# Attention ahead of two mixture-of-experts layers: the maxima are turned behind the next pair's scores, and the transfers and pieces around them move

## The chip, the cores and the metric

The kernel runs on one core of one Trainium2 chip. A core has five engines that run their own instruction lists: PE (TensorE, matrix products), DVE (VectorE), ACT (ScalarE), POOL (GpSimd) and SP (SyncE, which here issues nearly all DMA transfers, one behind the other). The metric is device time in microseconds (us) for one launch.

## The reference, cut to what matters

```python
scores = scale * np.matmul(q, k.transpose(0, 1, 3, 2))        # (4, 8, 576, 64) each
log_f = np.log(np.clip(f, 0.0001, 1.0))
cum = np.cumsum(log_f, axis=-1)
scores = np.where(causal, -1e9, scores + cum[:, :, :, None] - cum[:, :, None, :])
attn = np.exp(scores - np.max(scores, axis=-1, keepdims=True))
attn = attn / (np.sum(attn, axis=-1, keepdims=True) + 1e-09)
x = np.matmul(attn, v)              # put side by side to x: 2304 tokens x 512
h = (x @ w1) * (x @ w2) @ w3;  x = h @ w_out
e_idx = np.argmax(x @ w_gate, axis=1)      # then one of 8 experts per token,
out[mask] = gate_w * eom * (np.maximum(x[mask] @ w1[e], 0) @ w2[e])
```

## The kernel before

The 4 x 8 heads are taken as 16 pairs, n = 0 to 15; the two heads of a pair share the 128 partitions. All scores are computed twice. First as rows of queries, to find each query's largest score: the products x1, x3 and x2 (the last with x0 in its bank, all L217), and xl for the last 64 queries of both heads at once (L244, L245). DVE takes the largest of each tile into a column of M (L252; m1, m3, m2, m0 and, of xl, mL). PE then turns M (L259, the stage Tm, a product with the identity), ACT copies the nine rows to mt (L262, the stage tc), and SP writes them with two transfers as one row each per head, into MR (L183, 4 KB and 0.5 KB, the stage mv). Second, the scores are computed as columns of keys, in the banks gA to gD (L217); their last term, a product of MR and CK, brings in the maxima and the decay. ACT takes the exponent into PT (L289), POOL sets the causal part to zero (L295) and adds blocks up (L307), and PE multiplies by the values (v, L316) and sums up (L332).

Queries and keys are split into a high part (qh, kh: ACT, L203) and a low one (ql, kl: DVE, L210). The last 64 queries go through two small transfers (QD, from qh, the stage qd) into a block of their own for xl. For every pair SP also loads qr and kr (288 KB each), vr (320 KB), CK, the sums zd, and in pairs 4 to 11 clears rows of a table (xs from a tile of zeros, 771 KB, which POOL sets in pair 4).

Beside this, a weight piece per pair is brought in for the layers behind (w or wo, 512 KB), in seven steps c0 to c6: c0 loads, c1 is a copy on ACT (L469), c2, c3, c4 are integer operations on DVE (L471, L473, L475), c5 the high part on ACT (L478), c6 the low part on POOL (L480). A batch has four pairs; behind each batch the reciprocals of its sums are made (rv), stored, and, for the first batch, loaded again spread over partitions (rb, the stage xl of first_tile) and multiplied into xT on POOL (L367, the stage xm).

The order is written by hand. The table START gives a moment to each stage; stage x of pair n stands at START[x] + 9.8 n (PERIOD), SHIFT moves single ones, and all are sorted by this; every engine then carries out its own in this order. FILL adds products that nobody reads (fill, L162) behind a stage, to keep PE busy. On PE the order of a pair is: Tm, then x1, x3, x2 of the next pair, v and sums of the pair before, gA to gD, xl of the next pair, the first block of v. Behind attention come the dense and expert layers.

Of the kernel before, what the change touches and what calls it, by code (L numbers as in the profile page):

```python
# [11 lines left out]
F32 = mybir.dt.float32  # L12
F32R = mybir.dt.float32r
# [4 lines left out]
ACTF = mybir.ActivationFunctionType  # L18
# [4 lines left out]
B, H, S, D = 4, 8, 576, 64  # L23
NP = H // 2
N = B * S
DM = H * D
FF = 1024
E = 8
P = 128
# [18 lines left out]

PERIOD = 9.8
START = {  # L50
# [8 lines left out]
}  # L59
SHIFT = {}  # L60

FILL = {(0, "X0"): 5, (0, "XL"): 10, (1, "X0"): 4, (1, "XL"): 4, (2, "X2"): 5, (2, "X0"): 5}

AFTER = {
    "K4_13": 4.4, "K4_14": 4.43, "K0_15": 15.6, "K0_16": 15.61, "K0_17": 15.62, "inputs": 11.36, "scores": 13.38,
# [5 lines left out]
def spread(nc, d, rz):  # L71

    for h in range(2):
        nc.sync.dma_start(out=d[64 * h:64 * h + 64], in_=rz[h:h + 1].broadcast_to([64, rz.shape[1]]))


def attention(nc, tc, ident, xT, rz, xs, wc, q, k, v, f):
# [6 lines left out]
    V, A, G, PE, SP = nc.vector, nc.scalar, nc.gpsimd, nc.tensor, nc.sync  # L84
    with (
# [16 lines left out]

        def decay_parts():
            SP.dma_start(out=fc, in_=f)
            V.tensor_scalar(out=fc, in0=fc, scalar1=1e-4, scalar2=1.0, op0=ALU.max, op1=ALU.min)
            A.activation(out=fc, in_=fc, func=ACTF.Ln)
            V.tensor_tensor_scan(c8, fc, fc, 0.0, ALU.add, ALU.bypass)
            V.tensor_scalar(out=EK[0:NH], in0=c8, scalar1=-8.0, scalar2=None, op0=ALU.mult)
            V.scalar_tensor_tensor(out=EK[NH:], in0=c8, scalar=-8.0, in1=EK[0:NH].bitcast(F32), op0=ALU.mult, op1=ALU.subtract)
# [5 lines left out]
        OQ, OD = p1.tile([P, P], F32R, name="OQ"), p1.tile([P, P], F32R, name="OD")  # L115
        KHs = [[p2.tile([P, 640], F32R, name=f"{x}{i}", bufs=1) for i in range(2)] for x in ("kh", "kl")]
        QDs = [p1.tile([P, P], F32R, name=f"QD{i}") for i in range(2)]
        Ms = [p1.tile([P, 64], F32, name=f"M{i}") for i in range(2)]
        tri, tril = p1.tile([P, 640], F32, name="tri"), p1.tile([P, S], F32, name="tril")
        ones = p1.tile([P, 32], F32, name="ones")  # L120
        junk = p1.tile([P, S], F32, name="junk")
# [3 lines left out]
        def rows(e, t):  # L125
            e.memset(t.bitcast(F32), 0.0)
            for h in range(2):
                e.memset(t[64 * h:64 * h + 3, :min(S, t.shape[1])].bitcast(F32), 1.0)

        def constants():  # L130
            rows(G, CKs[0])
            rows(V, OQ)
            for t in (OD, *QDs, *[t[:, S:] for x in KHs for t in x]):
                V.memset(t.bitcast(F32), 0.0)
            for h in range(2):
                V.memset(OD[64 * h:64 * h + 3, HALF[h]].bitcast(F32), 1.0)
                for t in (OQ, OD):
                    V.memset(t[64 * h:64 * h + 1].bitcast(F32), 0.0)
            V.memset(ones, 1.0)
            for t in Ms:  # L140
                V.memset(t, 0.0)
            G.memset(tri, 0.0)
            G.affine_select(
                out=tri[:, 512:640], in_=tri[:, 512:640], pattern=[[-1, P]],
                compare_op=ALU.is_ge, fill=NEG, base=0, channel_multiplier=1,
            )
            G.memset(tril, 0.0)
            for h in range(2):
                G.affine_select(
                    out=tril[64 * h:64 * h + 64, 512:S], in_=tril[64 * h:64 * h + 64, 512:S],  # L150
                    pattern=[[-1, SL]], compare_op=ALU.is_ge, fill=NEG, base=0, channel_multiplier=1,
                )
            for t in MRs + CKs[1:]:
                rows(G, t)
# [3 lines left out]
        def fill(n):  # L158
            if n and "fill" not in st:
                st["fill"] = psv.tile([P, 1024], F32, name="fill", tag="v")  # L160
            for _ in range(n):
                PE.matmul(st["fill"][:, 0:512], z[:, :P], z, start=True, stop=True)  # L162
# [8 lines left out]
        st = {}  # L171

        def tl(s, key, shape, dt=F32, bufs=2):
            if key in ("kh", "kl"):
                s[key] = KHs[key == "kl"][s["n"] % 2]
                return s[key][:, :S]
            if key not in s:
                pool = p2 if key in ("qr", "kr", "kh", "kl", "qh", "ql") else p3
                s[key] = pool.tile([P, *shape], dt, name=f"{key}_{s['n']}", tag=key, bufs=bufs)
            return s[key]  # L180
# [75 lines left out]
                )  # L256

        def turn(s):
            PE.matmul(s["x", 4][0:64, 896:1024], Ms[s["n"] % 2], ident, start=True, stop=True)  # L259

        def turned(s):
            A.activation(out=tl(s, "mt", (P,), F32R)[0:9], in_=s["x", 4][0:9, 896:1024], func=ACTF.Copy)  # L262

        def spread_maxima(s):
            t, MR = s["mt"], MRs[s["n"] % 2]
# [93 lines left out]
                    SP.dma_start(out=view(rz), in_=z)  # L359

        def first_tile(s, x):
            for i in {7: (0, 1), 11: (2, 3)}.get(s["n"], ()):
                d = tl(s, f"rb{i % 2}", (512,), bufs=1)
                if x == 0:
                    spread(nc, d, rz[i, :, 0:512])
                else:
                    G.tensor_tensor(out=xT[:, i, 0:512], in0=xT[:, i, 0:512], in1=d, op=ALU.mult)  # L367

        def clear_rows(s):

            e = s["n"] - 4
            if 0 <= e < E:
                if e == 0:
                    zt = st["zt"] = p3.tile([P, DM + 2], F32, name="zero", bufs=1)
                    G.memset(zt, 0.0)
                    G.memset(zt[:, DM + 1:], float(2 * N))
                SP.dma_start(out=xs[e * N:e * N + W].rearrange("(c p) d -> p c d", p=P), in_=st["zt"].unsqueeze(1).broadcast_to([P, W // P, DM + 2]))

        stages = {
# [17 lines left out]
        for n in range(B * NP):  # L397
            st[n] = {"n": n}
        order = [(START[x] + SHIFT.get((n, x), 0.0) + PERIOD * n, n, i, x) for n in range(B * NP) for i, x in enumerate(START)]
        order = sorted(order + [(t + PERIOD * (B * NP - 1), B * NP, 0, x) for x, t in AFTER.items()])  # L400
        with tc.manual_schedule():
# [3 lines left out]
            for _, n, _, x in order:  # L405
# [14 lines left out]
                fn(st[n], *args)  # L420
                fill(FILL.get((n, x), 0))

# [839 lines left out]
def program(shapes):  # L1262
    nc = bacc.Bacc("TRN2", target_bir_lowering=False, num_devices=1)
    a = {n: nc.dram_tensor(n, s, mybir.dt.from_np(t), kind="ExternalInput").ap() for n, (s, t) in shapes.items()}
    out = nc.dram_tensor("out", (N, DM), F32, kind="ExternalOutput").ap()
    with tile.TileContext(nc) as tc:
        with tc.tile_pool(name="keep", bufs=1) as keep, tc.tile_pool(name="raws", bufs=2, reuse_waits="tile") as raws, tc.tile_pool(name="div", bufs=1, space=DRAM) as div:
            rz = div.tile([NP, 2, N], F32, name="rz")

            xs = div.tile([E * N, DM + 2], F32, name="xs")  # L1270
            ident = keep.tile([P, P], F32, name="ident")
            last = keep.tile([P, 64], F32, name="last")[:, :36]
            make_identity(nc, ident)
            xpool = ExitStack()
            xt = xpool.enter_context(tc.tile_pool(name="xt", bufs=1, side="right"))
            xT = xt.tile([P, NP, N], F32, name="xT")
            region = ExitStack()
            region.enter_context(tc.manual_schedule())
            wc = Combined(nc, tc, xpool, raws, a["wo"], a["w3t"], last)
            attention(nc, tc, ident, xT, rz, xs, wc, a["q"], a["k"], a["v"], a["f"])  # L1280
            moe(nc, tc, ident, xT, rz, xs, xpool, raws, region, wc, a["w1"], a["w2"], a["gates"], a["e1"], a["e2"], out)
            xpool.close()
    return nc
# [9 lines left out]
```

## Time and profile before

| | us |
|---|---|
| time, median of three runs (795.97, 795.99, 798.34) | 795.99 |
| the profiled execution | 797.8 |
| its span | 796.2 |
| PE busy in the span | 772.3 (97%) |
| DVE, ACT, POOL busy | 443.6, 276.3, 309.7 |
| mean granted TensorE clock, of full speed | 0.992 |

The profile is one execution; its span lies inside its time, 1.6 us shorter. The page gives shares of the whole span, so for attention, which fills the first 190 us, the questions have to be put to that stretch: how busy PE is in it, for what it waited, and when a certain product of each pair started. In a timeline row the columns are the start, the length, the engine, the line, the operation, what it writes from what it reads, and in brackets the idle time of the engine ahead of it and who ended that.

### The profile page before, as it was taken

What the parts mean: (1) busy time and instruction counts of PE and PEld (TensorE: products, weight loads), DVE (VectorE), ACT (ScalarE), POOL (GpSimd) and SP (SyncE); (2) the same over time, 40 slices, a digit from 0 to 9 for tenths busy, and PEclk for the clock granted to TensorE, in tenths of its full rate; (3) what the DMA queues carried; (4) which work ended last, traced back from release to release, by engine and by line L of the source; (5) the groups of instructions that cost most, each with busy time, mean ns of one, the idle gap of its engine ahead of it and who ended that gap; (6) DMA issues with size and microseconds to landing.
All of it is one profiled execution on the core that took longest, in us unless ns stands there. A gap on an engine that the chain in (4) does not pass through costs nothing. (4 is left out here: it accounts for less than half of the span.)

```text
span 796.2 us, 13782 instructions
## 1 busy us (share of the span) xinstructions
PE 772.3 (97%) x5153; PEld 643.9 (81%) x5155; DVE 443.6 (56%) x986; ACT 276.3 (35%) x537; POOL 309.7 (39%) x343
## 2 busy tenths in 40 slices
PE   7999999899999999999999999999999999999995
PEld 4676776677888887887888788898797999999983
DVE  7687887887989723341341322346478735445620
ACT  2565666564566222212221221313321222322221
POOL 6577888994000210230230111033444444444520
PEclk9999999999999999999999999999999999999998
DMA  3556777425635110110100010053676556456460
GB/s 108 158 150 195 230 230 249 147 86 168 201 123 196 53 42 28 40 40 5 55 16 13 21 40 0 4 189 112 215 231 221 165 189 229 146 185 214 146 262 30
DMA packets 40212, 102.12 MB, mean 128 GB/s; under 512 B 8611, under 2 KB 9315, under 8 KB 39889
## 3 DMA queue, kind: packets, MB, share of 16 engines
q1 hardware_dynamic: 36960, 91.46, 35.9%
q0 software_dynamic: 3184, 9.77, 3.2%
q8 instruction: 41, 0.67, 0.4%
q14 instruction: 27, 0.21, 0.1%
HBM read 84.47 MB, written 16.51 MB: 127 GB/s over the span
## 5 line engine op out<-in xcount | busy, mean ns | idle before, releaser
L595 DVE TENSOR_TENSOR ga<-b,ga 128x512 f32<-128x512 f32 (+1 forms) x40 | 25.4, 636 | 144.0 <-PE b L567 143.2
L726 POOL DMA_INDIRECT xs<-xr,pos x18 | 19.5, 1084 | 173.5 <-DVE pos L720 126.6
L252 DVE CUSTOM_DVE_ANT_0 junk<-x,tri 128x256 f32<-128x256 f32 (+3 forms) x128 | 62.9, 491 | 24.3 <-PE x L217 16.5
L565 PE MATMUL h<-gh,ah 128*128 128x320 f32 (+4 forms) x224 | 67.2, 300 | 0.0
L566 PE MATMUL h<-gl,ah 128*128 128x320 f32 (+4 forms) x224 | 66.9, 299 | 0.0
L567 PE MATMUL h<-gh,al 128*128 128x320 f32 (+4 forms) x224 | 66.9, 299 | 0.0
L565 PE MATMUL b<-xh,w2h 128*128 128x512 f32 (+1 forms) x160 | 59.9, 375 | 0.0
L565 PE MATMUL a<-xh,w1h 128*128 128x512 f32 (+1 forms) x160 | 59.8, 374 | 0.0
L567 PE MATMUL a<-xh,w1l 128*128 128x512 f32 (+1 forms) x160 | 58.9, 368 | 0.0
L567 PE MATMUL b<-xh,w2l 128*128 128x512 f32 (+1 forms) x160 | 58.9, 368 | 0.0
L566 PE MATMUL a<-xl,w1h 128*128 128x512 f32 (+1 forms) x160 | 58.8, 368 | 0.0
L566 PE MATMUL b<-xl,w2h 128*128 128x512 f32 (+1 forms) x160 | 58.8, 368 | 0.0
L565 PE MATMUL y<-raw,gh 128*128 128x512 f32 x144 | 56.9, 395 | 0.0
L567 PE MATMUL y<-raw,gl 128*128 128x512 f32 x144 | 56.2, 390 | 0.0
L566 PE MATMUL y<-raw,gh 128*128 128x512 f32 x144 | 56.0, 389 | 0.0
L295 POOL TENSOR_SCALAR_AFFINE_SELECT PT<-PT 128x256 f32<-128x256 f32 (+1 forms) x80 | 42.3, 547 | 35.3 <-ACT PT L289 35.3
L597 ACT ACTIVATE gh<-ga 128x512 fp32r<-128x512 f32 (+1 forms) x40 | 23.6, 589 | 87.3 <-DVE ga L595 87.3
L558 POOL TENSOR_SCALAR bh<-rb 128x1024 fp32r<-128x1024 f32 x28 | 37.0, 1324 | 42.9 <-DMA rb<-e 41.0
L1019 DVE SCALAR_TENSOR_TENSOR hl<-h,hh 128x320 fp32r<-128x320 f32 (+4 forms) x56 | 25.3, 461 | 46.8 <-ACT hh L1018 46.6
L316 PE MATMUL v<-PT,vr 128*64 128x448 f32 (+4 forms) x384 | 50.8, 402 | 0.0
L581 POOL TENSOR_TENSOR xT<-xT,rz 128x512 f32<-128x512 f32 (+1 forms) x16 | 19.8, 1235 | 76.6 <-ACT w2h L478 76.5
L559 DVE TENSOR_TENSOR bl<-rb,bh 128x1024 fp32r<-128x1024 f32 x28 | 37.0, 1338 | 15.0 <-POOL bh L558 15.0
(613 smaller groups left out, 2116.2 us busy)
## 6 DMA issues: line engine op xcount, KB each, us to landing
ra<-e SPq DMA_DIRECT2D x28, 512.0 KB
rb<-e SPq DMA_DIRECT2D x28, 512.0 KB
w<-w3t SPq DMA_DIRECT2D x16, 512.0 KB
xs<-zero SPq DMA_DIRECT2D x8, 771.0 KB
vr<-v SPq DMA_DIRECT2D x16, 320.0 KB
kr<-k SPq DMA_DIRECT2D x16, 288.0 KB
qr<-q SPq DMA_DIRECT2D x16, 288.0 KB
wo<-wo SPq DMA_DIRECT2D x8, 512.0 KB
```

The source lines that it names most:

```text
L252: V.tensor_tensor_reduce(out=junk[:, :w], in0=s["x", i][:, 512 * h:512 * h + w] if i < 4 else s["x", i][:, 224:224 + S], in1=tri[:, 640 - ...
L295: G.affine_select(out=t, in_=t, pattern=[[0, 2], [1, w]], compare_op=ALU.is_ge, fill=0.0, base=0, channel_multiplier=-1,)
L316: PE.matmul(s["v"][HALF[h], 384 + q0:384 + q1], s["vr"][:, j, HALF[h]], place(s, j, h, q0, q1), start=(j == 0), stop=(j == 4 or q1 == P),)
L558: G.tensor_scalar(out=hi, in0=src, scalar1=1.0, scalar2=1.0, op0=ALU.mult, op1=ALU.mult)
L559: lo_eng.tensor_tensor(out=lo, in0=src, in1=hi.bitcast(F32), op=ALU.subtract)
L565: PE.matmul(ps, ah, bh, start=start and i == 0, stop=False)
L566: PE.matmul(ps, ah, bl, start=False, stop=False)
L567: PE.matmul(ps, al, bh, start=False, stop=stop and i == last)
L581: G.tensor_tensor(out=xv, in0=xv, in1=d, op=ALU.mult)
L595: V.tensor_tensor(out=ga[:, :w], in0=pb[:, :w], in1=ga[:, :w], op=ALU.mult)
L597: A.activation(out=gh[:, f, :w], in_=ga[:, :w], func=ACTF.Copy)
L1019: V.scalar_tensor_tensor(out=hl[:, f, :w], in0=ps[:, :w], scalar=0.0, in1=hh[:, f, :w].bitcast(F32), op0=ALU.max, op1=ALU.subtract)
```

## The change

The turn of pair n moves behind x1, x3, x2 of pair n + 1 on PE and, for n from 1 to 14, writes into unused columns of the bank of that pair's x1 and no longer of its own xl. The QD transfers move in SP's order from behind the maxima's row to ahead of the load of vr, and so of the weight piece and of the row. c1 moves behind the turned maxima's copy, c2 one pair later; c5 comes ahead of that copy. The loads of rb and the multiplications of xT, two at pair 7 and two at 11, go one each to pairs 7 to 10; the tile of zeros is set at pair 2; the reciprocals (rv) move about half a pair later. At the start, constants are set in other gaps of DVE, ACT runs one Exp on a single column ahead of its first real one, mL of pair 0 goes ahead of m2 and m0, and the fillers lie elsewhere (34 and not 33).

```diff
--- before.py
+++ after.py
@@ -48,18 +48,18 @@
 
 PERIOD = 9.8
 START = {
-    "lk": -16.99, "c0": -13.79, "c1": -10.39, "lq": -9.49, "ck": -8.57, "kh": -7.55, "c2": -7.02, "qh": -6.92,
-    "X1": -5.99, "m1": -5.27, "X3": -5.12, "X2": -5.07, "m3": -2.49, "X0": -1.58, "m2": -1.5, "m0": -1.24, "qd": -0.95,
-    "kl": 1.21, "XL": 2.1, "mL": 3.54, "Tm": 3.61, "tc": 3.98, "ql": 1.3, "mv": 6.59, "cr": 7.59, "GA": 8.35,
+    "lk": -16.99, "c0": -13.79, "c1": -4.9, "lq": -9.49, "ck": -8.57, "kh": -7.55, "c2": 2.78, "qh": -6.92,
+    "X1": -5.99, "m1": -5.27, "X3": -5.12, "X2": -5.07, "m3": -2.49, "X0": -1.58, "m2": -1.5, "m0": -1.24, "qd": -4.8,
+    "kl": 1.21, "XL": 2.1, "mL": 3.54, "Tm": 4.8, "tc": 4.85, "ql": 1.3, "mv": 6.59, "cr": 7.59, "GA": 8.35,
     "HA": 8.43, "GB": 8.46, "HB": 8.5, "GC": 8.77, "HC": 9.64, "eA": 10.17, "eB": 10.24, "eC": 11.25, "GD": 11.28,
     "HD": 11.31, "a0": 11.0, "a1": 11.6, "a4": 11.7, "c3": 13.19, "eD": 13.33, "c4": 13.3, "c5": 14.02, "lv": 15.51,
     "s1": 13.9, "a2": 14.0, "a3": 14.1, "s2": 14.5, "c6": 17.0, "s3": 17.5, "p0": 22.91, "p1": 24.73,
-    "p3": 25.66, "su": 26.2, "xl": 33.6, "xa": 27.84, "sa": 28.24, "xm": 41.0, "zs": 32.77, "rl": 36.24, "rv": 57.6,
+    "p3": 25.66, "su": 26.2, "xl": 33.6, "xa": 27.84, "sa": 28.24, "xm": 43.2, "zs": 32.77, "rl": 36.24, "rv": 62.36,
     "rs": 63.34,
 }
-SHIFT = {}
-
-FILL = {(0, "X0"): 5, (0, "XL"): 10, (1, "X0"): 4, (1, "XL"): 4, (2, "X2"): 5, (2, "X0"): 5}
+SHIFT = {(0, "XL"): -4.55, (0, "mL"): -5.9, (0, "Tm"): -1.8, (0, "tc"): -1.8, (0, "mv"): -3.49}
+
+FILL = {(0, "XL"): 10, (1, "X0"): 2, (0, "HA"): 3, (0, "HB"): 5, (1, "XL"): 4, (2, "X0"): 5, (1, "HA"): 2, (1, "HB"): 3}
 
 AFTER = {
     "K4_13": 4.4, "K4_14": 4.43, "K0_15": 15.6, "K0_16": 15.61, "K0_17": 15.62, "inputs": 11.36, "scores": 13.38,
@@ -102,8 +102,11 @@
 
         def decay_parts():
             SP.dma_start(out=fc, in_=f)
+            small_constants()
             V.tensor_scalar(out=fc, in0=fc, scalar1=1e-4, scalar2=1.0, op0=ALU.max, op1=ALU.min)
             A.activation(out=fc, in_=fc, func=ACTF.Ln)
+            A.activation(out=junk[:, 0:1], in_=Ms[0][:, 0:1], func=ACTF.Exp)
+            pads()
             V.tensor_tensor_scan(c8, fc, fc, 0.0, ALU.add, ALU.bypass)
             V.tensor_scalar(out=EK[0:NH], in0=c8, scalar1=-8.0, scalar2=None, op0=ALU.mult)
             V.scalar_tensor_tensor(out=EK[NH:], in0=c8, scalar=-8.0, in1=EK[0:NH].bitcast(F32), op0=ALU.mult, op1=ALU.subtract)
@@ -127,18 +130,24 @@
             for h in range(2):
                 e.memset(t[64 * h:64 * h + 3, :min(S, t.shape[1])].bitcast(F32), 1.0)
 
+        def small_constants():
+            rows(V, OQ)
+            for h in range(2):
+                V.memset(OQ[64 * h:64 * h + 1].bitcast(F32), 0.0)
+            for t in Ms:
+                V.memset(t, 0.0)
+
+        def pads():
+            for t in (*QDs, *[t[:, S:] for x in KHs for t in x]):
+                V.memset(t.bitcast(F32), 0.0)
+
         def constants():
             rows(G, CKs[0])
-            rows(V, OQ)
-            for t in (OD, *QDs, *[t[:, S:] for x in KHs for t in x]):
-                V.memset(t.bitcast(F32), 0.0)
+            V.memset(OD.bitcast(F32), 0.0)
             for h in range(2):
                 V.memset(OD[64 * h:64 * h + 3, HALF[h]].bitcast(F32), 1.0)
-                for t in (OQ, OD):
-                    V.memset(t[64 * h:64 * h + 1].bitcast(F32), 0.0)
+                V.memset(OD[64 * h:64 * h + 1].bitcast(F32), 0.0)
             V.memset(ones, 1.0)
-            for t in Ms:
-                V.memset(t, 0.0)
             G.memset(tri, 0.0)
             G.affine_select(
                 out=tri[:, 512:640], in_=tri[:, 512:640], pattern=[[-1, P]],
@@ -256,10 +265,12 @@
                 )
 
         def turn(s):
-            PE.matmul(s["x", 4][0:64, 896:1024], Ms[s["n"] % 2], ident, start=True, stop=True)
+            x = st[s["n"] + 1]["x", 1][:, 256:] if 0 < s["n"] < B * NP - 1 else s["x", 4][:, 896:]
+            s["t"] = x[0:64, :P]
+            PE.matmul(s["t"], Ms[s["n"] % 2], ident, start=True, stop=True)
 
         def turned(s):
-            A.activation(out=tl(s, "mt", (P,), F32R)[0:9], in_=s["x", 4][0:9, 896:1024], func=ACTF.Copy)
+            A.activation(out=tl(s, "mt", (P,), F32R)[0:9], in_=s["t"][0:9], func=ACTF.Copy)
 
         def spread_maxima(s):
             t, MR = s["mt"], MRs[s["n"] % 2]
@@ -359,7 +370,7 @@
                     SP.dma_start(out=view(rz), in_=z)
 
         def first_tile(s, x):
-            for i in {7: (0, 1), 11: (2, 3)}.get(s["n"], ()):
+            for i in {7: (0,), 8: (1,), 9: (2,), 10: (3,)}.get(s["n"], ()):
                 d = tl(s, f"rb{i % 2}", (512,), bufs=1)
                 if x == 0:
                     spread(nc, d, rz[i, :, 0:512])
@@ -369,11 +380,11 @@
         def clear_rows(s):
 
             e = s["n"] - 4
+            if e == -2:
+                zt = st["zt"] = p3.tile([P, DM + 2], F32, name="zero", bufs=1)
+                G.memset(zt, 0.0)
+                G.memset(zt[:, DM + 1:], float(2 * N))
             if 0 <= e < E:
-                if e == 0:
-                    zt = st["zt"] = p3.tile([P, DM + 2], F32, name="zero", bufs=1)
-                    G.memset(zt, 0.0)
-                    G.memset(zt[:, DM + 1:], float(2 * N))
                 SP.dma_start(out=xs[e * N:e * N + W].rearrange("(c p) d -> p c d", p=P), in_=st["zt"].unsqueeze(1).broadcast_to([P, W // P, DM + 2]))
 
         stages = {
```

On PE, around the turn of pair 6 (x_7 are the next pair's tiles, v_1153 the output of the pair before); before:

```order
L316 MATMUL v_1153<-PT_958,vr_1042 64x128 x2
L316 MATMUL v_1153<-PT_958,vr_1042 64x448 x2
L259 MATMUL xl_1142<-ident,M_121 64x128
L217 MATMUL x_7_1164<-kh_116,qh_1151 128x256 x2
L217 MATMUL x_7_1164<-CK_109,OQ 128x256 x2
L217 MATMUL x_7_1178<-kh_116,qh_1151 128x512 x2
L217 MATMUL x_7_1178<-CK_109,OQ 128x512 x2
L217 MATMUL x_7_1184<-kh_116,qh_1151 128x384 x2
L217 MATMUL x_7_1184<-kh_116,qh_1151 128x128 x2
L217 MATMUL x_7_1184<-CK_109,OQ 128x384 x2
L217 MATMUL x_7_1184<-CK_109,OQ 128x128 x2
L316 MATMUL v_1153<-PT_958,vr_1042 64x448 x2
```

The same place after:

```order
L327 MATMUL v_1152<-PT_957,vr_1045 64x128 x2
L327 MATMUL v_1152<-PT_957,vr_1045 64x448 x2
L226 MATMUL x_7_1162<-kh_116,qh_1150 128x256 x2
L226 MATMUL x_7_1162<-CK_109,OQ 128x256 x2
L226 MATMUL x_7_1174<-kh_116,qh_1150 128x512 x2
L226 MATMUL x_7_1174<-CK_109,OQ 128x512 x2
L226 MATMUL x_7_1180<-kh_116,qh_1150 128x384 x2
L226 MATMUL x_7_1180<-kh_116,qh_1150 128x128 x2
L226 MATMUL x_7_1180<-CK_109,OQ 128x384 x2
L226 MATMUL x_7_1180<-CK_109,OQ 128x128 x2
L270 MATMUL x_7_1162<-ident,M_121 64x128
L327 MATMUL v_1152<-PT_957,vr_1045 64x448 x2
```

The turn (L259, now L270) has moved behind the three tiles and writes into the first of them.

On SP, from the load of pair 8's keys to that of the next queries; before:

```order
L188 DMA kr_1148<-k 128x576
L343 DMA zd<-zs_1088 2x2x288
L188 DMA vr_1197<-v 128x640
L462 DMA wo_1199<-wo 128x512
L183 DMA MR_111<-mt_1169 2x4x128
L183 DMA MR_111<-mt_1169 2x1x64
L352 DMA z_1215<-zd 128x1x36
L377 DMA xs<-zero 128x3x514
L183 DMA QD_120<-qh_1151 64x64 x2
L188 DMA qr_1268<-q 128x576
```

The same place after:

```order
L197 DMA kr_1147<-k 128x576
L354 DMA zd<-zs_1091 2x2x288
L192 DMA QD_120<-qh_1150 64x64 x2
L197 DMA vr_1200<-v 128x640
L473 DMA wo_1202<-wo 128x512
L192 DMA MR_111<-mt_1190 2x4x128
L192 DMA MR_111<-mt_1190 2x1x64
L363 DMA z_1218<-zd 128x1x36
L388 DMA xs<-zero 128x3x514
L197 DMA qr_1267<-q 128x576
```

The two QD transfers, which need qh, now stand ahead of vr, the piece and the row MR; behind the row only xs and, where there is one, z are left ahead of qr.

On DVE, pair 0's last maxima (x_0 are its tiles, M_121 its columns); before:

```order
L252 ISA junk,M_121<-x_0_226,tri 128x128
L252 ISA M_121 128x1
L252 ISA junk,M_121<-x_0_226,tri 128x128
L252 ISA M_121 128x1
L210 TENSOR_TENSOR kl_117<-kr_203,kh_115 128x576
L210 TENSOR_TENSOR ql_254<-qr_205,qh_212 128x576
L252 ISA junk,M_121<-xl_256,tril 128x576
L252 ISA M_121 128x1
L252 ISA junk,M_122<-x_1_278,tri 128x256
```

And after:

```order
L261 ISA junk,M_121<-xl_240,tril 128x576
L261 ISA M_121 128x1
L261 ISA junk,M_121<-x_0_227,tri 128x384
L261 ISA M_121 128x1
L261 ISA junk,M_121<-x_0_227,tri 128x384
L261 ISA M_121 128x1
L261 ISA junk,M_121<-x_0_227,tri 128x128
L261 ISA M_121 128x1
L261 ISA junk,M_121<-x_0_227,tri 128x128
L261 ISA M_121 128x1
L219 TENSOR_TENSOR kl_117<-kr_204,kh_115 128x576
L219 TENSOR_TENSOR ql_266<-qr_206,qh_213 128x576
```

The maximum of xl now comes ahead of four others, and kl and ql behind all of M.

## Rows read from the trace of the kernel before

**Rows 1.** Windows: stretch, length, busy time of each engine, clock, DMA share, GB/s.

```profile
200.00:500.00 300.00, 300.00 (x1369) 245.03 (x1368) 136.81 (x291) 89.65 (x170) 44.48 (x47) 1.00 0.17 57
```

**Rows 2.** Waits of PE in 0 to 200 us: total us, times, longest.

```profile
PE xl L259 <- DVE M L252: 4.8, 5, 1.9
PE xl L244 <- DMA QD<-qh: 2.4, 2, 1.9
```

**Rows 3.** Timeline of PE, the turns of pair 1 and of pair 15.

```profile
28.00 0.43 PE L259 MATMUL xl<-ident,M 128*64 128x128 f32 x2
...
172.19 0.27 PE L259 MATMUL xl<-ident,M 128*64 128x128 f32 x1
```

**Rows 4.** Timeline of PE, one pair from turn to turn.

```profile
80.00 0.38 PE L259 MATMUL xl<-ident,M 128*64 128x128 f32 x2
80.31 0.39 PE L217 MATMUL x<-kh,qh 64*128 64x256 f32 x2
...
81.74 1.95 PE L316 MATMUL v<-PT,vr 128*64 128x448 f32 x16
...
84.83 0.29 PE L217 MATMUL gA<-MR,CK 64*128 64x288 f32 x2
...
88.46 0.37 PE L244 MATMUL xl<-kh,QD 128*128 128x288 f32 x1 [0.53 <-DMA QD<-qh]
...
89.16 1.19 PE L316 MATMUL v<-PT,vr 128*64 128x128 f32 x8
90.18 0.38 PE L259 MATMUL xl<-ident,M 128*64 128x128 f32 x2
```

**Rows 5.** Windows of 4 us, and a timeline row of PE in the second.

```profile
24.00:28.00 4.00, 3.93 (x31) 3.05 (x28) 0.94 (x3) 2.76 (x4) 2.20 (x3) 0.75 0.86 285
68.00:72.00 4.00, 4.00 (x28) 2.38 (x27) 1.50 (x5) 2.38 (x4) 2.84 (x4) 0.71 0.89 275
...
68.37 2.15 PE L316 MATMUL v<-PT,vr 128*64 128x128 f32 x8
```

**Rows 6.** Timeline of SP and PE, the row of pair 10.

```profile
120.63 0.52 SPq L188 DMA_DIRECT2D vr<-v  x1
121.25 0.38 SPq L462 DMA_DIRECT2D w<-w3t  x1
121.72 1.19 SPq L183 DMA_DIRECT2D MR<-mt  x2
...
126.29 0.40 PE L217 MATMUL gA<-MR,CK 64*128 64x288 f32 x2 [1.11 <-DMA MR<-mt]
```

**Rows 7.** Timeline of SP and PE, pair 0 and the row's use in pair 1.

```profile
15.45 0.42 SPq L462 DMA_DIRECT2D wo<-wo  x1
17.20 1.16 SPq L183 DMA_DIRECT2D MR<-mt  x2
...
16.44 0.43 PE L259 MATMUL xl<-ident,M 128*64 128x128 f32 x2 [1.79 <-DVE M L252]
...
19.70 0.29 PE L217 MATMUL gA<-MR,CK 64*128 64x288 f32 x2
...
22.30 0.60 PE L217 MATMUL gC<-qh,kh 64*128 64x448 f32 x4 [1.59 <-DVE M L252]
...
32.54 0.30 PE L217 MATMUL gA<-MR,CK 64*128 64x288 f32 x2
```

**Rows 8.** Timeline rows of DVE, POOL and ACT.

```profile
14.29 0.75 DVE L210 TENSOR_TENSOR kl<-kr,kh 128x576 fp32r<-128x576 f32 x1
...
81.70 0.08 DVE L252 DVE_READ_ACCUMULATOR2_ANT M<- 128x1 f32 x1
...
129.91 2.53 POOL L367 TENSOR_TENSOR xT<-xT,rb 128x512 f32<-128x512 f32 x2
...
89.02 0.68 ACT L203 ACTIVATE qh<-qr 128x576 fp32r<-128x576 f32 x1 [0.48 <-DMA qr<-q]
```

**Rows 9.** Waits of SP in 0 to 200 us.

```profile
SPq L377 <- POOL zero L376: 3.3, 1, 3.3
```

## The prediction

> **What bounds the kernel now.** I read the stretches first, then what PE waited for, then one pair of heads closely. Between 200 and 500 us PE is busy for 300.00 of 300.00 us [rows 1], so what attention gains or loses before that shifts all that follows, one for one; the sum needs no later term. In the first 200 us PE is the engine to watch, and its waits are listed by cause: 4.8 us of the turn (Tm) for the maxima, 2.4 us of the last scores (xl) for the last queries' transfer [rows 2]. The pairs' own clock is the start of the turn: from 28.00 (pair 1) to 172.19 (pair 15) [rows 3], 144.19 us for 14 pairs, a mean of 10.30 us. A pair with little trouble shows what PE alone needs: turns at 80.00 and 90.18, less the 0.53 us in which xl waited, are 9.65 us apart [rows 4]. So 14 x 0.65 = 9.1 us in the pairs are stalls, and what follows from them. One thing follows that no list of waits names: behind the longer of the two waits for QD, 1.9 us with PE idle [rows 2], the granted clock is 0.71 over 68 to 72 us, part of the time thus 1.2 and not 2.4 GHz, and the first block of v takes 2.15 us [rows 5], where at full clock it took 1.19 [rows 4]. The start has the same: gC waits 1.59 us [rows 7], and 24 to 28 us run at 0.75 [rows 5].
>
> The figure to be moved is the profiled execution's 797.8 us; it lies 1.8 above the median of 795.99, and I take the sum off both.
>
> **The turn behind the next scores.** Before, a late maximum stopped PE with nothing else to do: up to 1.9 us [rows 2]. Now three score tiles, 1.43 us of PE work (80.31 to 81.74 [rows 4]), stand between. The turn now also waits for the maxima of the next pair's first tile, since it writes into that tile's bank. That tile's second half is read out at 81.70 + 0.08 [rows 8], 1.47 us behind the tile's start, so the turn comes some 0.05 us behind the third tile; with the signal to PE I take 0.1 us a pair, which makes the floor 9.75. x2 now waits for the last maximum itself, about 0.8 us behind where the turn stood, so lateness of DVE up to about that size is hidden, and of 1.9 us about 1.1 would be left. Also, DVE loses a loop: before, the next maxima could not start until the turn and the first tile had been through PE; now they only need the tile. The price is on the row's way back. From turn to the first product that reads the row (gA with MR) there were 4.83 us (80.00 to 84.83 [rows 4]); now 4.83 - 1.43 = 3.40. The copy and SP's issue begin 0.76 us behind the turn (16.44 to 17.20), and the row was there 2.50 us later at the latest (19.70, no wait shown) [rows 7]: 3.26 of 3.40. So alone it fits, by little.
>
> **Queries' transfers ahead of the row.** The 1.9 us wait came of SP standing 3.3 us behind the clearing of a tile on POOL with the two QD transfers queued behind it [rows 9]; that clearing moves two pairs earlier and QD no longer stands behind it. The 0.53 us go too. I book both, and the half-clock stretch, as gone; they are inside the 10.30. But QD's new place is a wait in SP's order: SP stands until ACT has made the next queries (qh), and vr, the weight piece (w) and the row queue behind that. Count from gA's product with the row, U = 84.83. qh ran 89.02 to 89.70 with 0.48 of waiting for its input [rows 8], which QD's leaving moves forward; so it is done at U+4.39. Two QD issues take as long as the row's two, 1.16 us [rows 7]; then vr, and w starts at about U+6.1 (vr's issue runs 0.52 [rows 6]). The turn, before at U+4.82 without the 0.53, comes at U+6.35, the row's issue at U+7.1. Thus 832 KB leave SP 1.0 to 1.6 us ahead of 4.5 KB that PE is waiting for.
>
> What does the row cost there? No row of before has just this; three bound it. Its own time, 2.50 behind its issue: U+9.6, no stall. Behind one piece, wo issued at 15.45 and the row in use at 19.70, 4.25 us [rows 7]: U+10.35 at the latest. And the one pair where vr, w and the row went out at 120.63, 121.25 and 121.72: gA waited 1.11 us and got the row at 126.29, 5.04 behind w [rows 6]: U+11.1, though there four rb transfers had gone out just before, and now at most two do. I take U+10.15, between the floor of 9.75 and 10.35 and nearer the latter, since vr goes out too, and the row at 15.45 shows no wait. Pieces stand ahead of the row in about 12 pairs; in the last ones no w does. 12 x 10.15 + 2 x 9.75 = 141.3 against 144.19: **2.9 us gained**. With no stall 14 x 9.75 = 136.5: 7.7 gained. At 11.1, 152.7: 8.5 lost.
>
> The Trainium skill (DMA: Bandwidth & Descriptors, section Queues, rings and completion order) says that each of the 16 DMA engines consumes a queue's descriptors in order, and that a transfer's semaphore is written only after all earlier writes of that DMA engine. The waiting row at 126.29 agrees; by the rule the row would never land before w's share on its DMA engines, and the sum would lie at the upper two bounds, not at U+9.6.
>
> **Pieces, multiplications, reciprocal.** c1 leaves the place ahead of PT<-gA, c2 goes one pair later: the same number of ACT and DVE instructions per pair in other gaps, off PE's path; I book zero (if c5, now ahead of mt, were late, the row would be late by as much, at most its own 0.6). Two xT multiplications at once kept POOL for 2.53 us [rows 8], behind which DVE's maxima were late for the turn's 1.9; one each in pairs 7 to 10 is 1.26 a pair. POOL is then close to full in four pairs, and I keep the 0.05 to 0.45 a pair by which it might limit (at most 1.8 us) for the range. The two rb issues fall into SP's wait for qh.
>
> **Start-up.** The last maximum of pair 0 is taken ahead of two others, and kl and ql behind all of them, so the turn no longer waits for these two, 0.75 us each [rows 8] with some overlap, some 1.35 together: 16.44 becomes 15.1. gC of pair 0 waits for pair 1's maxima, whose chain starts as much earlier: 22.30 becomes 20.95. Fillers between gA, gB and gC (eight of them) now keep PE busy through most of what was the 1.59 us hole, so I take the half-clock stretch behind it as gone. Its price is the excess of the one like it: v's 2.15 against 1.19 makes 1.0, and the four xl products ahead of it some 0.5 more; I take 1.3. The turn of pair 1, at 28.00 before, would so come at 25.35, and at 26.8 behind its three tiles; the row is there 3.26 later by its own time, 30.1, where before it was used at 32.54 [rows 7]: **2.4 us gained**. If the row waits for w there too, 1.4; 2.7 with the whole 1.5 of the clock. The Exp table's load leaves PT<-gA's head for a gap at the start; it is no term, since gC waits for the maxima. The sum: 2.9 + 2.4 = 5.3 us, so 792.5 for the profiled execution and **790.7** for the median.
>
> **Rivals.** *The row in time*: transfers overlap so that the row passes w. For it: 3.26 of 3.40 us [rows 7]. Against it: 126.29, and the rule. 7.7 + 2.7 = 10.4 gained, 785.6. *The row behind vr and w in every pair*, the mechanism by which the change loses: gA waits for the row, so kh, qh, QD, vr and w all come later by as much, and the loop closes over SP's queue, not over PE. At 4.65 behind w, the middle of the two bounds, the period is 10.75: 12 x 10.75 + 19.5 = 148.5, 4.3 lost; start-up gives 1.8, and PE's idle 1.5 to 2 us ahead of gA of pair 1 would cost another half-clock stretch, 1.5: 4.0 lost, 800; by the upper bound 804. It decides from 12P + 19.5 = 144.19 + 2.4, P = 10.59, the row 4.5 behind w. By the skill's rule this has more weight than the row in time. *The stalls of the maxima stay*, because POOL and DVE hinder each other in pairs 7 to 10 and the first tile's maximum, now in the turn's way, is late: the change doesn't do what it says. Then some 3 us of turn waits come back, and 2 us are left: 794.
>
> **How the numbers follow.** Forecast 0.42 (788.5 to 793.5), row in time 0.20 (785.6), row late 0.23 (796 to 804), stalls stay 0.15 (792.5 to 796). About 0.3%, 2.4 us, can be told from no change. Faster: 0.36 of the forecast, 0.20, 0.05 of the last, 0.61. Same: 0.06, 0.06 of the late row, 0.09: 0.21. Slower: 0.17, 0.01: 0.18. The range leaves out the worst of the late row and the best of the full gain: 784.5 to 799.5.
>
> **What the profile will show.** Right: turns 10.0 to 10.3 us apart; PE's waits with "DMA MR" in many pairs, 0.2 to 0.7 us each; no wait for QD; no clock under 1.00 at 64 to 72; gC of pair 0 at about 21, gA with the row of pair 1 near 30. Row in time: no MR waits, 9.75. Row late: MR waits of 0.8 us and more in the pairs with a piece, turns 10.6 and more apart, perhaps a low clock near 30. Stalls stay: turn or x2 waits for DVE M. Wrong altogether: a wait of gA for kl or ql, or of vr or zd on SP, which I hold for hidden.

## The result

The changed kernel is slower: 806.5 us median against 796.05, a ratio of 1.0121 (95% interval 1.0097 to 1.0146; a ratio here and below goes by all fast executions of both kernels, not by the two medians). Its profiled execution took 804.73 us, 6.9 more than that of before, with a span of 803.1; the comparison of the two traces goes by these two executions. The forecast was 790.7, faster.

PE's waits in the first 220 us of the changed kernel, beside [rows 2] (columns as there):

```profile
PE gA L226 <- DMA MR<-mt: 7.1, 6, 2.5
PE x L270 <- DVE M L261: 1.7, 2, 0.9
...
PE xl L253 <- DMA QD<-qh: 0.8, 1, 0.8
PE xl L270 <- DVE M L261: 0.8, 1, 0.8
```

The waits that were to go are mostly gone: the turn waits 2.5 us for maxima (4.8 before), 0.8 of it in pair 0 and 1.7 in two new places; xl waits for QD only in pair 0. What came in their place is 7.1 us of gA for the row of maxima, 4.5 of it in two pairs. The turns, as in [rows 3], timeline of PE; the first two and the last are those of pairs 1, 2 and 15:

```profile
27.36 0.43 PE L270 MATMUL x<-ident,M 128*64 128x128 f32 x2
...
39.12 0.32 PE L270 MATMUL x<-ident,M 128*64 128x128 f32 x1
...
49.75 0.32 PE L270 MATMUL x<-ident,M 128*64 128x128 f32 x1
...
53.35 0.40 PE L226 MATMUL gA<-MR,CK 64*128 64x288 f32 x2
...
59.83 0.32 PE L270 MATMUL x<-ident,M 128*64 128x128 f32 x1
...
112.50 0.32 PE L270 MATMUL x<-ident,M 128*64 128x128 f32 x1 [0.74 <-DVE M L261]
...
117.92 0.40 PE L226 MATMUL gA<-MR,CK 64*128 64x288 f32 x2 [1.96 <-DMA MR<-mt]
...
125.97 0.32 PE L270 MATMUL x<-ident,M 128*64 128x128 f32 x1
...
157.60 0.32 PE L270 MATMUL x<-ident,M 128*64 128x128 f32 x1 [0.95 <-DVE M L261]
...
163.59 0.40 PE L226 MATMUL gA<-MR,CK 64*128 64x288 f32 x2 [2.51 <-DMA MR<-mt]
...
171.66 0.32 PE L270 MATMUL x<-ident,M 128*64 128x128 f32 x1
...
179.74 0.27 PE L270 MATMUL xl<-ident,M 128*64 128x128 f32 x1
```

An ordinary pair takes 10.08 us (49.75 to 59.83), near the forecast. Some 0.30 us of it is the row: the product that reads it starts 0.43 us behind gA's product before it (52.92), where e3 below has 0.13; the list names no wait there. But from pair 9 to pair 10 it is 13.47, and from 13 to 14 it is 14.06: two pairs lose 7.4 us against 10.1, and 0.74 and 0.95 more just ahead of them. The turn of pair 15 comes at 179.74, 7.55 behind [rows 3]. At both places the clock falls behind the hole (windows; the column behind POOL's is the granted clock):

```profile
120.00:124.00 4.00, 4.00 (x32) 3.31 (x30) 0.57 (x1) 3.05 (x4) 2.48 (x3) 0.64 0.61 198
...
164.00:168.00 4.00, 4.00 (x38) 3.82 (x38) 1.23 (x2) 2.13 (x3) 0.70 (x1) 0.59 0.02 8
```

What made the row late there is in SP's timeline ahead of 117.92:

```profile
106.79 0.53 SPq L354 DMA_DIRECT2D zd<-zs  x1
111.72 0.63 SPq L370 DMA_DIRECT2D rz<-z  x1
112.45 1.16 SPq L192 DMA_DIRECT2D QD<-qh  x2
...
114.30 0.41 SPq L473 DMA_DIRECT2D w<-w3t  x1
114.81 1.20 SPq L192 DMA_DIRECT2D MR<-mt  x2
```

And in DVE's, from the end of the last maximum on:

```profile
109.72 1.55 DVE L367 TENSOR_SCALAR z<-z 128x36 f32<-128x36 f32 x1
111.31 0.38 DVE L368 RECIPROCAL z<-z 128x36 f32<-128x36 f32 x1
```

SP issues zd at 106.79 and then stands until 111.72 at rz, the store of the first batch's reciprocals, which DVE makes at 111.31, right behind the last maximum. QD, vr, w and the row all queue behind it. The list of SP's waits has it, though it names the DVE maximum beside the reciprocal and not the reciprocal, whose result the store reads:

```profile
SPq L370 <- DVE M L261: 9.0, 2, 4.6
```

The change moved the reciprocals (rv, from 57.6 to 62.36) and left their store (rs, 63.34) where it was.

### The profile page after: what moved, and what is told of

Same layout as the page of the kernel before. It is cut to its first block, busy times and chain, and to the rows that moved or that the text cites. A ratio compares the mean times of both kernels' runs of the same rounds, so it can differ in the third digit from the quotient of the medians.

```text
span 803.1 us, 13792 instructions
## 1 busy us (share of the span) xinstructions
PE 777.9 (97%) x5156; PEld 650.7 (81%) x5156; DVE 445.4 (55%) x986; ACT 280.4 (35%) x538; POOL 305.9 (38%) x343
## 5 line engine op out<-in xcount | busy, mean ns | idle before, releaser
L306 POOL TENSOR_SCALAR_AFFINE_SELECT PT<-PT 128x256 f32<-128x256 f32 (+1 forms) x80 | 37.5, 488 | 45.2 <-ACT PT L300 43.3
L592 POOL TENSOR_TENSOR xT<-xT,rz 128x512 f32<-128x512 f32 (+1 forms) x16 | 21.6, 1348 | 79.6 <-ACT w2h L489 79.6
L569 POOL TENSOR_SCALAR bh<-rb 128x1024 fp32r<-128x1024 f32 x28 | 33.6, 1202 | 45.8 <-DMA rb<-e 38.1
```

The costliest lines, as they stand in the source:

```text
L306: G.affine_select(out=t, in_=t, pattern=[[0, 2], [1, w]], compare_op=ALU.is_ge, fill=0.0, base=0, channel_multiplier=-1,)
L569: G.tensor_scalar(out=hi, in0=src, scalar1=1.0, scalar2=1.0, op0=ALU.mult, op1=ALU.mult)
L592: G.tensor_tensor(out=xv, in0=xv, in1=d, op=ALU.mult)
```

## The experiments

Theory A says that this queue behind the store is the loss; theory B, that the row behind vr and w in every pair is. Ratios are to the kernel before, timed beside each, with the 95% interval; of each edit the lines that matter are shown, cut to the numbers changed.

**e1**, the changed kernel with the reciprocals back:

```diff
-"rv": 62.36
+"rv": 57.6
```

> The changed kernel with the reciprocals back where they stood (rv 57.6 and not 62.36); all else as changed. Theory A (the queue): SP stood up to 4.6 us at the store of the reciprocals, in pairs 9 and 13, with QD, vr, the piece and the row of maxima behind it; what followed there (0.74 and 0.95 us at the turn, 1.96 and 2.51 at gA, and a half-clock stretch of about 1.3 to 1.5 us behind each) goes: 8 to 9 us off 806.5, so about 798. Theory B (the row behind w in every pair is the loss, and these two pairs only show it most): at most 3 us, 803 or more.

Measured: 1.0016 (0.9998 to 1.0034), by the ratios some 8.4 us less than the changed kernel's 1.0121. The waits for the row fall to 4.2 us, and the turns at the two places wait for DVE no more. PE's waits:

```profile
PE gA L226 <- DMA MR<-mt: 4.2, 5, 1.3
```

Theory A holds for nearly all of the loss; B's bound of 3 us is passed.

**e2**, the reciprocals late as changed, their store behind the row:

```diff
-"rs": 63.34
+"rs": 65.5
```

> The changed kernel with the reciprocals late as changed, but their store on SP (rs 65.5 and not 63.34) behind the row of maxima. Theory A: SP no longer waits with the row behind it; only what the late reciprocal costs on DVE stays (the turn's 0.74 and 0.95 us in two pairs): 799 to 800. If it is the place of the reciprocal on DVE, behind the last maximum and ahead of the next, that makes the row late, nothing is gained: 806.

Measured: 1.0026 (1.0012 to 1.0039). With DVE's order untouched and only SP's changed, nearly the same is regained. What stays is the turn's wait, as expected: 1.9 us in two places (PE's waits).

```profile
PE x L270 <- DVE M L261: 1.9, 2, 1.2
PE gA L226 <- DMA MR<-mt: 1.8, 3, 1.1
```

**e4**, the kernel before with the reciprocals alone moved:

```diff
-"rv": 57.6
+"rv": 62.36
```

> The kernel before with the reciprocals alone moved late (rv 62.36). Theory A: SP stands at their store ahead of vr, the piece and the row here too, so gA waits for the row in pairs 9 and 13, some 1.5 to 3 us each with perhaps a half-clock stretch: 799 to 803. If it hurts only together with QD's new place: 796.

Measured: 1.0088 (1.0056 to 1.0119). The same one number costs some 7 us in the kernel before (by the interval 4.5 to 9.5), with QD elsewhere and the turn in its old place; SP waits 9.9 us at two stores (its waits, then PE's):

```profile
SPq L359 <- DVE M L252: 9.9, 2, 5.4
```

```profile
PE gA L217 <- DMA MR<-mt: 4.2, 2, 2.2
```

So A needs none of the change's other parts. It also leaves the question why the rest, e1, gains nothing.

**e3**, as e1, with the queries' transfers behind vr and the piece, still ahead of the row:

```diff
-"qd": -4.8
+"qd": -3.9
-"rv": 62.36
+"rv": 57.6
```

> As e1, and the queries' transfers (qd -3.9 and not -4.8) behind vr and the piece, still ahead of the row. Theory B's step (the row lands with w, and w is late because QD waits for qh ahead of it): vr goes out about 2.5 and w about 1.5 us earlier, the row lands by its own time, pairs take about 9.75 and not 10.1 us: 4 us less than e1, about 794. If the row is late by its own chain (turn, copy, issue) and not by w: the same as e1, about 798. If QD, now issued just ahead of the row, delays it: slower than e1.

Measured: 0.9955 (0.9935 to 0.9975). The place of the two QD transfers makes 4.9 us, as theory B asked: the row no longer keeps anyone (0.2 us, in pair 1), and an ordinary pair takes 9.70. PE's waits, then its timeline:

```profile
PE gA L226 <- DMA MR<-mt: 0.2, 1, 0.2
```

```profile
58.00 0.32 PE L270 MATMUL x<-ident,M 128*64 128x128 f32 x1
...
67.70 0.32 PE L270 MATMUL x<-ident,M 128*64 128x128 f32 x1
...
86.87 0.38 PE L226 MATMUL x<-kh,qh 64*128 64x256 f32 x2 [0.98 <-ACT qh L212]
```

So both theories hold, each for its own part. The last row is a third thing: in pair 7 the next scores wait for qh.

**e12**, as e1, with the piece's load behind the row:

```diff
-"c0": -13.79
+"c0": -12.9
-"rv": 62.36
+"rv": 57.6
```

> As e1, with the weight piece's load (c0 -12.9 and not -13.79) behind the row of maxima; QD still waits for qh ahead of vr and the row. If it is the piece's 512 KB ahead of the row that makes it late: gA's waits for the row (4.2 us in e1) go, as in e3 where the piece went out earlier, and the time is that of e3, 0.9955. If vr's 320 KB alone keep the row late, or the turn's own lateness does: 1.000, as e1 (1.0016). If the piece, now later and next to xs, becomes late itself for ACT and DVE: above 1.002.

Measured: 1.023 (1.0209 to 1.0251), the slowest of all, by a way that I had only half in view. The row's waits do go, 4.2 to 0.5 us, with QD's wait and vr still ahead of it: it was the piece's 512 KB. But the piece now goes out just ahead of xs and qr, and qr, not the piece itself, is what comes late. PE's waits, then SP's and ACT's timelines in one pair:

```profile
PE x L226 <- ACT qh L212: 11.9, 8, 2.3
...
PE gA L226 <- DMA MR<-mt: 0.5, 2, 0.3
```

```profile
87.08 0.34 SPq L473 DMA_DIRECT2D wo<-wo  x1
...
88.20 0.45 SPq L388 DMA_DIRECT2D xs<-zero  x1
88.71 0.48 SPq L197 DMA_DIRECT2D qr<-q  x1
```

```profile
94.85 0.68 ACT L212 ACTIVATE qh<-qr 128x576 fp32r<-128x576 f32 x1 [2.46 <-DMA qr<-q]
```

qr, issued at 88.71 behind 512 and 771 KB, is used at 94.85, 6.1 us later; QD and everything behind wait with it. The clock falls behind these waits, too: its mean is 0.980, where e1 has 0.997. Since PE waits for qh from pair 5 on, the row has more time there; what tells of the piece are pairs 2 to 4, ahead of the first xs: their turns are 9.71 and 9.79 us apart (38.94, 48.65, 58.44) and gA doesn't wait, against 10.07 and 9.87 in e1.

**e5**, as e3, with the clearing transfer xs behind qr, and pair 1's fillers out:

```diff
-"cr": 7.59
+"cr": 10.3
-(1, "HA"): 2, (1, "HB"): 3
```

> As e3, the clearing transfer xs (cr 10.3 and not 7.59) behind the load of the next queries, not ahead of it, and without the five fillers behind gA and gB of pair 1. What e3 still shows: in pair 7 the next scores wait 0.98 us for qh and 0.41 behind it, since qr goes out behind xs (771 KB). If qr is late because of xs: these 1.4 us and some 0.4 of the like in pair 10 go, and the fillers' 1.2 us, about 2.5 us less than e3: 0.9925 of the kernel before, or 790. If xs in its new place delays CK, kr, or vr and w and with them the row: no better than e3 (0.9955) or worse.

Measured: 0.991 (0.9892 to 0.9929), 790.2 us: the fastest, faster than both kernels. No wait for qh is left in the list of PE's waits.

**e10**, as e3, with e5's place of xs alone:

```diff
-"cr": 7.59
+"cr": 10.3
```

> As e3, with the clearing transfer behind the queries' load, the fillers of pair 1 left in: one of the two edits of e5 alone. If both edits carry their part (1.8 and 1.2 us): 0.993. If the fillers were all: 0.9955.

Measured: 0.9938 (0.9925 to 0.9951). The wait for qh in pair 7 is gone (0.38 us for CK stands there instead); the fillers would be worth the rest, 0.9938 to 0.991, though these two intervals overlap. The traces agree: from the turn of pair 1 to that of pair 2 e10 takes 10.60 us (27.42 to 38.02) and e5 9.17 (27.45 to 36.62).

**e8**, as e3, with the turn back in its old place and bank (the lines on the bank and on pair 0 in SHIFT are left out here):

```diff
-"Tm": 4.8, "tc": 4.85
+"Tm": 3.61, "tc": 3.98
```

> As e3, with the turn back ahead of the next scores (Tm 3.61, tc 3.98, into xl's own bank). If the turn's move is what takes the waits for the maxima (4.8 us in the kernel before, 1.8 of it at the start): some 3 us slower than e3, 0.999. If those waits come of POOL and DVE in pairs 7 to 11 and go with the spread of the multiplications: no slower than e3, 0.9955.

Measured: 0.9957 (0.9939 to 0.9976), the same as e3. The time is that of the second reading, but the trace doesn't show its mechanism: with the multiplications spread, e8 has 4.5 us of turn waits, 3.5 of them behind pair 0 (3.0 of 4.8 in the kernel before), and the longest is one of pair 13:

```profile
148.16 0.43 PE L270 MATMUL xl<-ident,M 128*64 128x128 f32 x2 [2.24 <-DVE M L261]
```

In e3 0.5 us are left, so it is the turn's move that takes them. e8 pays for these waits and for ordinary pairs of 9.93 us, not 9.70, but it lacks e3's 1.4 us in pair 7 (0.98 for qh, 0.41 behind it); the rest of the balance is not laid out.

**e9**, e5 with the turn back (cut as in e8):

```diff
-"Tm": 4.8, "tc": 4.85
+"Tm": 3.61, "tc": 3.98
```

> As e5, with the turn back ahead of the next scores, as in e8. e8 against e3 said that the turn's move gains nothing on the whole (0.9957 and 0.9955): what it takes from the waits for maxima it adds as 0.1 us a pair and as waits for ACT. If so, the same as e5, 0.991, or 0.989, since the row then has 1.4 us more. If with the queries' loads in time the turn's move does pay: slower than e5, 0.994.

Measured: 0.9955 (0.9938 to 0.9973) against e5's 0.991. With the queries in time the turn's move does pay, 0.45%. Two turns in PE's timeline, of e9, then of e5:

```profile
64.88 0.43 PE L270 MATMUL xl<-ident,M 128*64 128x128 f32 x2
...
74.81 0.43 PE L270 MATMUL xl<-ident,M 128*64 128x128 f32 x2
```

```profile
46.32 0.32 PE L270 MATMUL x<-ident,M 128*64 128x128 f32 x1
...
56.02 0.32 PE L270 MATMUL x<-ident,M 128*64 128x128 f32 x1
```

9.93 against 9.70 a pair. And e9 has e8's wait of 2.24 us in pair 13, of which e5 keeps about half, 0.81 at x2 and 0.25 at the turn behind it (PE's timeline of e5):

```profile
145.58 0.50 PE L226 MATMUL x<-kh,qh 64*128 64x384 f32 x4 [0.81 <-DVE M L261]
```

Why an ordinary pair takes 9.93: in e8 DVE ends the last maximum at 64.81 + 0.08, the turn follows at 64.94, and DVE idles 0.99 us until the turn and the first tile have been through PE. Without that loop, in e5, PE shows no wait in such a pair (DVE's timeline of e8):

```profile
64.81 0.08 DVE L261 DVE_READ_ACCUMULATOR2_ANT M<- 128x1 f32 x1
65.88 0.42 DVE L261 CUSTOM_DVE_ANT_0 junk<-x,tri 128x256 f32<-128x256 f32 x1 [0.99 <-PE x L226]
```

**e6**, the kernel before with the start-up part alone (SHIFT, FILL, constants, early Exp):

> The kernel before with the start-up part of the change alone (constants in other gaps, early Exp, pair 0's last maximum ahead of two others, fillers moved); turn, transfers, pieces, reciprocals and multiplications as before. The prediction's term: 2.4 us gained, 0.997, gC of pair 0 at about 21 and no half clock at 24 to 28 us. If the hole only moves on to pair 1 (its fillers cost 1.2 us, or a wait for the row follows): 0.999 to 1.000.

Measured: 1.0005 (0.9988 to 1.0022). The turn of pair 1 comes at 26.20 and not 28.00, without the low clock at 24 to 28 us (1.00 against 0.75 in [rows 5]). But the low clock does not come with every execution of the old start. e4's start is that of the kernel before, from 8.8 us on its products up to gC begin within 0.03 us of the same times, gC waits as long ([rows 7]), and yet (timeline of PE and window of e4):

```profile
22.30 0.50 PE L217 MATMUL gC<-qh,kh 64*128 64x448 f32 x4 [1.60 <-DVE M L252]
...
24.00:28.00 4.00, 3.93 (x37) 2.83 (x36) 1.39 (x5) 3.13 (x5) 3.13 (x5) 1.00 0.86 280
...
26.41 0.43 PE L259 MATMUL xl<-ident,M 128*64 128x128 f32 x2
```

Against that execution the new start gains 0.2 us and not 1.8, which by itself fits the 1.0005. In e6's own profiled execution the turn of pair 15 stands at 172.01, against 172.19 in [rows 3]; of its 1.8 us 0.6 are gone by pair 12, and 1.1 go behind the turn that waits for the maxima near 142 us, where the clock falls (timeline of PE, then the window):

```profile
141.70 0.69 PE L270 MATMUL xl<-ident,M 128*64 128x128 f32 x2 [1.95 <-DVE M L261]
```

```profile
140.00:144.00 4.00, 2.30 (x12) 1.77 (x14) 2.39 (x8) 0.79 (x2) 4.00 (x6) 0.71 0.43 152
```

In the kernel before the same stretch shows 1.00, behind a hole of the same size (1.93 us at 142.89, the longest of the five in [rows 2]). These are single executions; that the clock falls there in each of e6's is not shown.

**e7**, as e3, with the pieces' first steps back:

```diff
-"c1": -4.9
-"c2": 2.78
+"c1": -10.39
+"c2": -7.02
```

> As e3, with the pieces' first steps back where they stood (c1 -10.39, c2 -7.02). The prediction's term: zero, 0.9955 as e3. If the copy c1, again ahead of PT<-gA on ACT, makes the exponents and so qh late, or c5 behind mt makes nothing better: slower than e3, 0.997 or more.

Measured: 0.9946 (0.9927 to 0.9964), as e3 within the intervals: no price of the pieces is seen, as the term of zero said.

**e11**, the kernel before with QD alone moved:

```diff
-"qd": -0.95
+"qd": -3.9
```

> The kernel before with the queries' transfers alone moved, behind the piece and ahead of the row (qd -3.9). If the wait of 1.9 us at xl, its half-clock stretch of 1.5 and the 0.5 us at pair 7 came of QD standing behind xs: 3 to 4 us less, 0.9955 to 0.996. If xs, which still waits 3.3 us for the zeros from POOL, now holds up qr and with it qh instead: 0.998 to 1.000.

Measured: 0.9985 (0.9971 to 1.0000), 1.2 us and the upper of the two expectations. The waits for QD are gone; SP still stands 3.3 us at xs for the zeros, and now qr behind it is late, so that the scores wait 0.59 us and 0.41 more where xl had waited 1.9 (timeline of PE):

```profile
68.41 0.39 PE L217 MATMUL x<-kh,qh 64*128 64x256 f32 x2 [0.59 <-ACT qh L203]
```

## Why the prediction was wrong

- **The step that failed** is in the part on pieces, multiplications and reciprocal. The heading names the reciprocal; the text puts no price on it. The sum took rv's move for nothing, on DVE, where it costs 1.9 us (e2). What had to be asked is who waits for it: the store rz, on SP, with QD, vr, the piece and the row queued behind. The diff had both numbers, 62.36 for the reciprocals and 63.34 for the store, one microsecond apart in the plan where it had been nearly six. e1, e2 and e4 put 7 to 8.4 us on it, more than the whole forecast gain of 5.3. The sentence on what would prove me wrong held waits of vr and zd on SP for hidden and did not think of rz, which stands between them.
- **What the store doesn't explain.** Without it e1 still gains nothing (1.0016), where 5.3 us were forecast: its turn of pair 15 stands at 172.89, 0.7 us behind [rows 3]. Found in its trace are the start-up's 2.4 us, used up by pair 2 (below), 1.35 us in pair 7 (0.94 for qh and 0.41 behind it) and 1.1 us for the maxima in pair 12 (0.86 at x2, 0.26 at the turn). The rest is not laid out.
- **The row behind vr and w** was right in mechanism and, on the whole, in size. Forecast was U+10.15, a price of 0.40 us in 12 pairs, 4.8 in all; moving QD takes 4.9 us off (e1 to e3). It is not spread as forecast: by the start of the product that reads the row, as in the result, the changed kernel loses 0.11 to 0.30 us in pairs 3 to 8, but 1.6 and 0.8 in pairs 1 and 2. The rule of the Trainium skill (DMA: Bandwidth & Descriptors, section Queues, rings and completion order) named in the prediction agrees with e3 and e12: with the piece earlier or later, the row's waits fall from 4.2 to 0.2 and 0.5 us. That a pair would take 9.75 without it was right, too: 9.70 in e3 and e5.
- **The rival of the row late in every pair** was forecast to lose by a period above 10.59. An ordinary pair stayed under that; the time came out on its side, mostly by another mechanism. Nor did the half-clock stretch come that it priced near 30 us: behind the row's wait of 1.38 us in pair 1 the clock is 1.00 over 28 to 36 us. The row in time, the first rival, is what e3 shows, with QD's wait out of the piece's way. That lateness comes over SP's queue was the right picture, with the wrong head of the queue.
- **The stalls of the maxima.** The prediction laid the turn's 1.9 us to two multiplications at once and booked it as gone with their spread. e8 and e9 don't bear that out: with one a pair, 2.24 us stand one pair later. The turn's move takes about 1.2 of that (e5), somewhat more than the 0.8 worked out.
- **QD's waits** went, as booked, but that QD's leaving moves qr forward was only half of it. In pair 7, z and xs still go out ahead of qr. In the changed kernel qr's issue itself lasts 1.97 us there, and qh comes late (timelines of SP and of ACT):

```profile
83.56 1.97 SPq L197 DMA_DIRECT2D qr<-q  x1
```

```profile
88.80 0.68 ACT L212 ACTIVATE qh<-qr 128x576 fp32r<-128x576 f32 x1 [1.29 <-DMA qr<-q]
```

  The pair takes 11.36 us, 1.2 more than its neighbours. e11 and e10 show the same from both sides.
- **The turn's move.** The 0.1 us a pair and the loop that DVE loses were right; e9 against e5 gives it 0.45%. In the changed kernel an ordinary pair is longer than e9's 9.93, by the row; what the turn's move gains there was not tried alone.
- **Start-up.** Forecast were the turn of pair 0 at 15.1, gC at 20.95 at full clock, the row of pair 1 in use at 30.1. Measured (timeline of PE):

```profile
15.30 0.43 PE L270 MATMUL xl<-ident,M 128*64 128x128 f32 x2 [0.78 <-DVE M L261]
...
21.54 0.50 PE L226 MATMUL gC<-qh,kh 64*128 64x448 f32 x4
...
30.96 0.40 PE L226 MATMUL gA<-MR,CK 64*128 64x288 f32 x2 [1.38 <-DMA MR<-mt]
```

  1.6 us gained of 2.4, the row behind w once more, near the 1.4 that the prediction gave for that case. Then five fillers stand between gA and gC of pair 1 that the working never priced: 1.4 us (e10 against e5). The next turn is at 39.12. In the kernel before it was at 37.65, a pair's 9.65 behind 28.00, and three tiles later, where the turn now stands, that is 39.08: the term was used up within one pair. And 1.3 us of the term's working were the price of a low clock that was read from one execution and that e4, with the same start, lacks.
- **Pieces, multiplications**: zero was right for the pieces (e7). The multiplications were not tried alone; with their spread e8 has no fewer turn waits behind pair 0 than the kernel before.

## What to carry to other kernels

When a step is moved, list who waits for its result, and on which in-order queue that waiter stands; price the whole queue behind it, not the step. Look for what goes out just ahead of a small transfer that an engine waits for (here 4.5 KB about a microsecond behind 832, worth 4.9 us), and for what is put behind it instead: e12 cured the row and, against e1, lost 17 us on qr. Of several edits that belong together, one can hide the gain of another: the turn's move was worth nothing on e3, with the queries late, and 0.45% on e5. And a term that comes of the clock in one profiled execution should be read in a second one before it is booked.

## What the runs showed that I had not expected

The clock does not follow the hole's length alone, nor the program: with the same start, a wait of gC of 1.59 us is followed by 0.75 in the kernel before and one of 1.60 by 1.00 in e4. Near 142 us a wait of 1.93 us left the clock at 1.00 in the kernel before and one of 1.95 is followed by 0.71 in e6; behind e8's 2.24 us it stays at 1.00. So one microsecond gained ahead of such a hole can be given back behind it, or not, from one execution to the next. And the DVE operation on 36 columns ahead of the reciprocal took 1.55 us at 109.72, where it took 0.69 in the kernel before (at 105.19). In both it ends 0.04 to 0.05 us behind a POOL addition that runs beside it (109.13 to 111.23, and 104.81 to 105.83); that this is the cause was not tried.
